# Agent attention with two expert layers: five weight buffers and six value buffers in place of four and seven, first queries loaded among the keys

## The chip, the cores and the metric

One core of one Trainium2 chip runs the kernel in one launch. The metric is the device time of that core in microseconds (us), the median of several runs. The engines are called PE (matrix multiplies, with its weight loads listed as PEld), DVE (vector), ACT (scalar), POOL (GpSimd) and SP (here only an issuer of transfers). Transfers are also issued from POOL and from ACT.

## What is computed

49 agents attend over 12,480 keys, then 12,480 queries attend over the agents, and the result runs through two expert layers with a squared ReLU. In short, with N = 12480, C = 128 and a hidden width of 2048:

```python
def sm(a, b):
    s = scale * (a @ b.T)
    e = np.exp(s - s.max(-1, keepdims=True))
    return e / (e.sum(-1, keepdims=True) + 1e-09)
agent_v = sm(agents, k) @ v                # 49 x 128
x = sm(q, agents) @ agent_v                # 12480 x 128
r = np.maximum(x @ w_in, 0.0)              # 12480 x 2048
x = (moe_s * (r * r) + moe_b) @ w_out
h = np.maximum(x @ w_in2, 0.0)
out = (h * h @ w_out2)
```

q, k, v and the agents are 32-bit floats, the weights 64-bit floats. [...]

## The kernel before

Everything is written in one hand-made order (`tc.manual_schedule`): the order of the Python statements is the order of the instructions on each engine, and the order of the transfers on each issuer.

The kernel has four stages.

- **Keys** (the loop `for g in range(NG + 1)`). The 12,480 keys come in 13 groups, twelve of 1024 rows (512 KB) and a last one of 192 rows. In step g, `k_transpose(g)` turns group g on PE (L412) and ACT copies the result (L414), `k_scores(g - 1)` multiplies by the agents on PE (L422) and ACT copies the scores into S (L424), and `k_max(g - 2)` keeps a running maximum on DVE (L428). `k_load(g + KB - 1)` issues the key group five ahead from SP (L369); KB = 6 buffers hold raw keys.
- **The maximum** (from `k_max(NG - 1)`): DVE reduces the running maximum (L452), then in the order of PE's queue come `q_transpose(0)` (L145), the transpose of the maximum (L456), `q_transpose(1)`, a small multiply that spreads the maximum to all partitions (L464). DVE copies its result to `mb` (L466).
- **Values** (the loop with L507): per group, DVE subtracts `mb` from S (L490), ACT takes the exponential (L491), PE multiplies by the value group. `v_upto(min(g + VB, NG))` issues further value groups from SP (L376). A value group lies in buffer `v_buf[g % VB]`.
- **Experts**: 28 blocks of queries, 8 steps a block, from about 75 us to the end.

Weights are 16 chunks of 512 KB, numbered w0 to w15 here. `w_load` (L251 for two of the matrices, L256 for the other two) brings a chunk into one of RAW buffers, `w_decode` takes it apart with an ACT instruction (L268) and DVE instructions (L270 to L285) that stand between the instructions of the other stages: `fill(n)` puts n of them in. A chunk's raw buffer is free after L280. `next_load()` issues the next chunk from POOL when a decoding has ended, as far as `fill` counts. So the raw buffers say how many chunks are on their way ahead of the decoder.

`FIRST` is the string that lists the first transfers of SP's queue, "k" for a key group and "w" for a weight chunk; there are as many "w" as raw buffers. After it, SP's transfers come as the loops write them: before the change k6 in step 1, k7 in step 2 and so on to k12 in step 7, v0 in step 7, v1 in step 8, q0, q1 and v2 in step 9, v3 to v6 in steps 10 to 13, and the others in the value loop. In step 2, ACT issues two small broadcasts, `s_sb` and `b_sb`.

Of the kernel before, what the change touches and what calls it, by code (L numbers as in the profile page):

```python
# [18 lines left out]
BP = 112  # L19
LAG = 2  # L20
WC = 512
RAW = 4
KB = 6
VB = 7
FIRST = "kkwkwkwkwk"

FILL_K = (1, 3, 4, 4, 4, 5, 5, 5, 5, 5, 5, 4, 1, 0)
FILL_T = 1
# [15 lines left out]
def tile_agent_attention_two_moe(  # L44
# [40 lines left out]
    def rows_of(x, piece):  # L85
        t, p, j = piece
        return x[t:t + p * j, :].rearrange("(p j) c -> p j c", j=j)
# [34 lines left out]
    def tokens_of(x, t):  # L122

        t0, p, j = blocks[t]
        if t < DIRECT:
            return rows_of(x, blocks[t])
        return x[t0:t0 + p * j, :].rearrange("(j p) c -> p j c", j=j)

    def q_load(t):
        t0, p, j = blocks[t]  # L130
        q_raw[t] = qp.tile([P, 512], F32, tag="q_raw", name="q_raw", bufs=3)
        if t < DIRECT:
            nc.sync.dma_start(out=q_raw[t].rearrange("p (j c) -> p j c", c=C)[:p, :j], in_=tokens_of(q, t))
        else:
            with nc.allow_non_contiguous_dma(reason="channels on the partitions"):
                nc.sync.dma_start(out=q_raw[t][:, :p * j], in_=q[t0:t0 + p * j, :].rearrange("t c -> c t"))
# [105 lines left out]

    raw_p = ctx.enter_context(tc.tile_pool(name="raw_p", bufs=RAW))
    dec_p = ctx.enter_context(tc.tile_pool(name="dec_p", bufs=3))
# [61 lines left out]
    def fill(n):  # L306

        for _ in range(n):
            if len(running) < 2 and ready and (not running or running[0][1] >= 3):
                running.append([ready.pop(0), 0])  # L310
            if not ready and loaded and (not running or running[-1][1] >= ZA):
                raw, i, pair = loaded.pop(0)
                sl = slice(i * WC, (i + 1) * WC)
                g = w_decode(raw, pair[0][:, sl], pair[1][:, sl])
                next(g)
                ready.append(g)
            if not running and ready:
                running.append([ready.pop(0), 0])
            if not running:
                while late:  # L320
                    late.pop(0)[1]()
                    undone[0] -= 1
                return
            for x in late:
                x[0] -= 1
            while late and late[0][0] <= 0:
                late.pop(0)[1]()
                undone[0] -= 1
            r = running.pop(0)
            r[1] += 1  # L330
            try:
                next(r[0])
                running.append(r)
            except StopIteration:
                done.append(0)
            for i in range(len(done)):
                done[i] += 1
            if done and done[0] > 2:
                done.pop(0)
                next_load()  # L340
# [14 lines left out]
    with tc.manual_schedule():  # L355

        with tc.tile_pool(name="pre", bufs=1) as pre, tc.tile_pool(name="kp", bufs=2) as kp:
            NG = len(kblocks)
            ag = pre.tile([NA, C], F32, name="ag")
            vs = {}  # L360
            v_buf = [pre.tile([P, 8, C + 1], F32, name=f"v{i}") for i in range(VB)]
            S = pre.tile([P, NT, NA], F32, name="S")
# [3 lines left out]
            def k_load(g):  # L366
                _, p, j = kblocks[g]
                kraw[g] = kp.tile([P, 8, C], F32, tag="kraw", name="kraw", bufs=KB)
                nc.sync.dma_start(out=kraw[g][:p, :j], in_=rows_of(k, kblocks[g]))  # L369

            def v_upto(n):
                while len(vs) < n:
                    g = len(vs)
                    _, p, j = kblocks[g]
                    vs[g] = v_buf[g % VB]
                    nc.sync.dma_start(out=vs[g][:p, :j, :C], in_=rows_of(v, kblocks[g]))  # L376
# [11 lines left out]
            for x in Xs:  # L388
                nc.gpsimd.memset(x.bitcast(F32), 0.0)
            for what in FIRST:  # L390
                if what == "k":
# [15 lines left out]
            def k_transpose(g):  # L407
                _, p, j = kblocks[g]
                x = kraw.pop(g)
                ps = ps_h.tile([P, 1024], F32, tag="h", name="ps_k")  # L410
                for i in range(j):
                    nc.tensor.transpose(out=ps[:, i * p:(i + 1) * p], in_=x[:p, i], identity=ident[:p, :p])  # L412
                kT[g] = kp.tile([P, 1024], F32, tag="kT", name="kT")
                nc.scalar.copy(kT[g][:, :p * j], ps[:, :p * j])  # L414

            def k_scores(g):
                _, p, j = kblocks[g]
                x = kT.pop(g)
                ps = ps_m.tile([P, 512], F32, tag="m", name="ps_ks")
                sc = ps[:p, :j * GAP].rearrange("p (j n) -> p j n", n=GAP)  # L420
                for i in range(j):
                    nc.tensor.matmul(out=sc[:, i], lhsT=x[:, i * p:(i + 1) * p], rhs=aT, start=True, stop=True)  # L422
                to = S[:p, t0[g]:t0[g] + j]
                nc.scalar.copy(to, sc[:, :, :NA])  # L424

            def k_max(g):
                _, p, j = kblocks[g]
                nc.vector.tensor_tensor(  # L428
                    out=mxa[:p, :j], in0=S[:p, t0[g]:t0[g] + j], in1=(mxa if g > 1 else S)[:p, :j], op=ALU.max
                )  # L430

            for g in range(NG + 1):
                if g < NG:
                    k_transpose(g)
                if g and g + KB - 1 < NG:
                    k_load(g + KB - 1)
                if g == 2:
                    nc.scalar.dma_start(out=s_sb, in_=s.partition_broadcast(P))
                    nc.scalar.dma_start(out=b_sb, in_=b.partition_broadcast(P))
                if g == 9:  # L440
                    q_load(0)
                    q_load(1)
                v_upto(min(g - KB, VB))
                fill(FILL_K[g])
                if g:
                    k_scores(g - 1)
                if g > 2:
                    k_max(g - 2)
# [43 lines left out]

            v_upto(VB)
            for g in range(3):
# [4 lines left out]
            for g, (_, p, j) in enumerate(kblocks):  # L499
# [6 lines left out]
                for i in range(j):  # L506
# [6 lines left out]
                    )  # L513
                v_upto(min(g + VB, NG))
                fill(FILL_V[g])
# [190 lines left out]
```

## Time and profile before

| what | value |
|---|---|
| median of three runs | 1127.05 us (1122.84, 1127.05 and 1130.47) |
| the profiled execution | 1124.37 us, of it a span of 1122.4 us from the first to the last instruction |
| busy shares of the span | PE 99%, PEld 91%, DVE 86%, ACT 85%, POOL 1% |
| keys, PE | from 5.2 to 39.9 us |
| values, PE | from 46.5 to 70.6 us |
| expert stage | from 75.3 us to the end |
| transfers of the first 73 us | 16 weight chunks, 13 key groups, 13 value groups, 5 query blocks |

The span is counted from the first instruction. A transfer's "landing" is the time from its issue on the queue until its completion is seen. An idle time in a row of the timeline is the time that the engine stood still ahead of that row, with what ended it. The share of a clock of 1.00 is TensorE's upper level of 2.4 GHz, 0.50 its lower level of 1.2 GHz.

### The profile page before, as it was taken

What the parts mean: (1) busy time and instruction counts of PE and PEld (TensorE: products, weight loads), DVE (VectorE), ACT (ScalarE), POOL (GpSimd) and SP (SyncE); (2) the same over time, 40 slices, a digit from 0 to 9 for tenths busy, and PEclk for the clock granted to TensorE, in tenths of its full rate; (3) what the DMA queues carried; (4) which work ended last, traced back from release to release, by engine and by line L of the source; (5) the groups of instructions that cost most, each with busy time, mean ns of one, the idle gap of its engine ahead of it and who ended that gap; (6) DMA issues with size and microseconds to landing.
All of it is one profiled execution on the core that took longest, in us unless ns stands there. A gap on an engine that the chain in (4) does not pass through costs nothing.

```text
span 1122.4 us, 15479 instructions
## 1 busy us (share of the span) xinstructions
PE 1105.9 (99%) x5787; PEld 1021.1 (91%) x5787; DVE 964.3 (86%) x1426; ACT 949.8 (85%) x1196; POOL 12.4 (1%) x36
## 2 busy tenths in 40 slices
PE   9988999999999999999999999999999999999998
PEld 8877999999999999999999999999999999999997
DVE  6889888888888888888888888888888888888876
ACT  6669888888888888888888888888888888888876
POOL 2100000000000000000000000000000000000000
PEclk9899999999999999999999999999999999999999
DMA  9960039999999999999999999999999999800000
GB/s 343 291 166 1 1 19 7 15 15 15 7 16 15 16 9 14 15 15 15 8 15 15 15 8 15 15 15 8 15 15 15 8 15 15 12 1 9 9 10 15
DMA packets 1282674, 34.96 MB, mean 31 GB/s; under 512 B 1255255, under 2 KB 1277672, under 8 KB 1282600
## 3 DMA queue, kind: packets, MB, share of 16 engines
q1 hardware_dynamic: 1280320, 27.56, 116.1%
q0 software_dynamic: 1728, 6.29, 1.7%
q8 instruction: 45, 0.74, 0.4%
q14 instruction: 29, 0.24, 0.2%
q10 hardware_dynamic: 552, 0.12, 0.1%
HBM read 27.58 MB, written 6.39 MB: 30 GB/s over the span
## 4 chain that ended last, share of the span: by engine, by line
PE 93%; DMA 3%; DVE 1%; ACT 1%; issue 0%; SPq 0%; DVEq 0%; ACTq 0%
PE ps_y L584 47%; PE ps_h L572 24%; PE ps_h L562 16%; PE ps_av L507 2%; DMA kraw<-in_k_dram 2%; DMA q_raw<-in_q_dram 2%; PE ps_o L623 1%; PE ps_sT L181 1%; PE ps_x L227 0%; DVE gl L117 0%; PE ps_b L196 0%; PE ps_s L171 0%; ACT r L551 0%; PE ps_q L145 0%; ACT r L552 0%
## 5 line engine op out<-in xcount | busy, mean ns | idle before, releaser
L117 DVE TENSOR_TENSOR gl<-r,gh 128x896 fp32r<-128x896 f32 (+2 forms) x450 | 487.7, 1084 | 16.8 <-ACT gh L116 1.5
L551 ACT ACTIVATE r<-ps_h 128x896 f32<-128x896 f32 (+2 forms) x450 | 408.9, 909 | 98.8 <-PE ps_h L562 79.7
L552 ACT ACTIVATE r<-r 128x896 f32<-128x896 f32 (+2 forms) x450 | 427.0, 949 | 14.3
L116 DVE CAST gh<-r 128x896 fp32r<-128x896 f32 (+2 forms) x445 | 276.7, 622 | 112.5 <-ACT r L552 100.6
L562 PE MATMUL ps_h<-X,Ml 113*128 113x448 f32 (+1 forms) x448 | 166.5, 372 | 2.5 <-DVE X L238 1.7
L572 PE MATMUL ps_h<-yh,wi2l 128*128 128x448 f32 (+1 forms) x448 | 168.8, 377 | 0.2 <-ACT r L551 0.2
L584 PE MATMUL ps_y<-gh,wol 128*128 128x448 f32 (+1 forms) x448 | 163.0, 364 | 0.9 <-ACT y L592 0.9
L562 PE MATMUL ps_h<-X,Mh 113*128 113x448 f32 (+1 forms) x448 | 163.5, 365 | 0.0
L584 PE MATMUL ps_y<-gl,woh 128*128 128x448 f32 (+1 forms) x448 | 162.6, 363 | 0.6 <-DVE gl L117 0.6
L572 PE MATMUL ps_h<-yl,wi2h 128*128 128x448 f32 (+1 forms) x448 | 163.2, 364 | 0.0
L572 PE MATMUL ps_h<-yh,wi2h 128*128 128x448 f32 (+1 forms) x448 | 163.2, 364 | 0.0
L584 PE MATMUL ps_y<-gl,wo2h 128*128 128x448 f32 (+1 forms) x448 | 162.4, 362 | 0.1
L584 PE MATMUL ps_y<-gh,woh 128*128 128x448 f32 (+1 forms) x448 | 162.4, 362 | 0.0
L584 PE MATMUL ps_y<-gh,wo2l 128*128 128x448 f32 (+1 forms) x448 | 162.3, 362 | 0.0
L584 PE MATMUL ps_y<-gh,wo2h 128*128 128x448 f32 (+1 forms) x448 | 161.8, 361 | 0.0
L562 PEld LDWEIGHTS ps_h<-X,Ml 113*128 113x128 f32 x448 | 84.3, 188 | 9.3 <-issue 3.3
L584 PEld LDWEIGHTS ps_y<-gh,wol 128*128 128x128 f32 x448 | 84.4, 188 | 7.3 <-ACT y L592 1.2
L572 PEld LDWEIGHTS ps_h<-yl,wi2h 128*128 128x128 f32 x448 | 84.8, 189 | 6.5 <-DVE yl L117 0.2
L584 PEld LDWEIGHTS ps_y<-gl,woh 128*128 128x128 f32 x448 | 84.4, 188 | 6.7 <-DVE gl L117 0.9
L572 PEld LDWEIGHTS ps_h<-yh,wi2h 128*128 128x128 f32 x448 | 84.1, 188 | 7.0
L572 PEld LDWEIGHTS ps_h<-yh,wi2l 128*128 128x128 f32 x448 | 84.2, 188 | 6.7 <-ACT r L551 0.5
L562 PEld LDWEIGHTS ps_h<-X,Mh 113*128 113x128 f32 x448 | 84.9, 190 | 5.2
(125 smaller groups left out, 975.6 us busy)
## 6 DMA issues: line engine op xcount, KB each, us to landing
kraw<-in_k_dram SPq DMA_DIRECT2D x12, 512.0 KB, 11.6
v<-in_v_dram SPq DMA_DIRECT2D x12, 512.0 KB, 7.9
q_raw<-in_q_dram SPq DMA_DIRECT2D x27, 224.0 KB, 36.3
out_dram<-o SPq DMA_DIRECT2D x27, 224.0 KB, 2.8
raw<-in_moe_w_out_dram POOLq DMA_DIRECT2D x8, 512.0 KB, 8.3
raw<-in_moe_w_in_dram SPq DMA_DIRECT2D x4, 512.0 KB, 8.1
raw<-in_moe_w_in_dram POOLq DMA_DIRECT2D x4, 512.0 KB, 8.0
q_raw<-in_q_dram SPq DMA_DIRECT2D x1, 192.0 KB, 31.7
```

The lines of the kernel that those rows point to most:

```text
L116: copy(dst[0], src)
L117: eng_lo.tensor_tensor(out=dst[1], in0=src, in1=dst[0].bitcast(F32), op=ALU.subtract)
L181: nc.tensor.matmul(out=ps[:KS, :n], lhsT=aS, rhs=x[z][:, :n], start=(z == 1), stop=(z == 0))
L507: nc.tensor.matmul(out=ps_av[:NA, :C + 1], lhsT=S[:p, t0[g] + i], rhs=vs[g][:p, i], start=(g == 0 and i == 0), stop=(g == NG - 1 and i == ...
L551: nc.scalar.activation(r[:, c, :n], ps[:, c, :n], AF.Relu)
L552: nc.scalar.activation(r[:, c, :n], r[:, c, :n], AF.Square)
L562: nc.tensor.matmul(out=ps[:, c, :n], lhsT=M[z][:KS, sl], rhs=X[t], start=(z == 1), stop=(z == 0))
L572: nc.tensor.matmul(out=ps[:, c, :n], lhsT=w[:, sl], rhs=y[:, :n], start=(z == 0), stop=(z == 2))
L584: nc.tensor.matmul(out=py[t][:, :n], lhsT=wz[:, m], rhs=g[:, c, :n], start=(m == 0 and z == 0), stop=(m == NCH - 1 and z == 2),)
L623: nc.tensor.transpose(out=po[:, i], in_=x[:, (h * jh + i) * p:(h * jh + i + 1) * p], identity=ident)
```

## The change

Three constants and two lines of the key loop are edited. RAW goes from 4 to 5 and `FIRST` gets an eleventh entry, a fifth weight chunk (w4) behind k5; it was the first chunk that POOL issued, and POOL now begins with w5. VB goes from 7 to 6. In the key loop the values are issued two steps sooner, one a step from step 5 on (v0) to step 10 (v5), and the two first query blocks in steps 7 and 8 in place of both in step 9.

```diff
-RAW = 4
+RAW = 5
 KB = 6
-VB = 7
-FIRST = "kkwkwkwkwk"
+VB = 6
+FIRST = "kkwkwkwkwkw"
@@ in the key loop
-                if g == 9:
-                    q_load(0)
-                    q_load(1)
-                v_upto(min(g - KB, VB))
+                if g in (7, 8):
+                    q_load(g - 7)
+                v_upto(min(g - 4, VB))
```

SP's order of transfers, before and after (step numbers in brackets):

```
before: k0 k1 w0 k2 w1 k3 w2 k4 w3 k5    [1]k6 [2]k7 [3]k8 [4]k9 [5]k10 [6]k11 [7]k12 v0 [8]v1 [9]q0 q1 v2 [10]v3 ...
after:  k0 k1 w0 k2 w1 k3 w2 k4 w3 k5 w4 [1]k6 [2]k7 [3]k8 [4]k9 [5]k10 v0 [6]k11 v1 [7]k12 q0 v2 [8]q1 v3 [9]v4 [10]v5
```

The order of the decoding instructions among the others on DVE and ACT is the same in both kernels: it depends on `fill`'s numbers, and a loaded chunk is at hand for it in the list with four as with five.

## Rows read from the trace of the kernel before

**Rows 1.** Busy time of each engine by stretch, with TensorE's granted clock
```profile
core 0: us, PE busy (x) PEld busy (x) DVE busy (x) ACT busy (x) POOL busy (x), PEclk, DMA share, GB/s
20.00:23.73 3.73, 2.82 (x26) 2.71 (x25) 1.65 (x5) 0.75 (x2) 0.35 (x1) 1.00 1.03 384
...
40.00:42.00 2.00, 0.00 (x0) 0.00 (x0) 1.74 (x4) 0.23 (x2) 0.00 (x0) 1.00 1.20 267
43.30:50.10 6.80, 6.77 (x31) 6.10 (x32) 5.36 (x16) 3.46 (x7) 0.00 (x0) 0.50 1.04 278
...
100.00:1100.00 1000.00, 998.99 (x5058) 922.92 (x5057) 869.07 (x1227) 870.69 (x1070) 0.00 (x0) 1.00 1.26 12
```

**Rows 2.** Timeline of PE: start, duration, line, operation, count, idle before
```profile
20.02 1.06 PE L412 MATMUL ps_k<-ident,kraw 128*128 128x128 f32 x8
...
23.73 1.07 PE L412 MATMUL ps_k<-ident,kraw 128*128 128x128 f32 x8 [0.91 <-DMA kraw<-in_k_dram]
...
34.86 1.05 PE L412 MATMUL ps_k<-ident,kraw 128*128 128x128 f32 x8
...
37.48 0.34 PE L412 MATMUL ps_k<-ident,kraw 96*128 96x96 f32 x2
...
42.04 0.57 PE L145 MATMUL ps_q<-ident,q_raw 112*128 112x112 f32 x4 [2.13 <-DMA q_raw<-in_q_dram]
...
44.15 0.66 PE L464 MATMUL ps_mb<-dm,ones_r 49*128 49x49 f32 x2
...
54.06 16.58 PE L507 MATMUL ps_av<-v,S 128*49 128x129 f32 x148
```

**Rows 3.** Timeline of SP: issues of the key groups 7, 8 and 12
```profile
8.67 0.33 SPq L369 DMA_DIRECT2D kraw<-in_k_dram  x1
...
12.50 0.33 SPq L369 DMA_DIRECT2D kraw<-in_k_dram  x1
...
21.12 0.34 SPq L369 DMA_DIRECT2D kraw<-in_k_dram  x1
```

**Rows 4.** Transfers by issue: the same three groups, with us to landing
```profile
kraw<-in_k_dram SPq DMA_DIRECT2D x1, 512.0 KB, 14.9
...
kraw<-in_k_dram SPq DMA_DIRECT2D x1, 512.0 KB, 13.9
...
kraw<-in_k_dram SPq DMA_DIRECT2D x1, 96.0 KB, 12.5
```

**Rows 5.** Waits of SP's queue, 9 to 14 us: total, times, longest
```profile
SPq L369 <- DMA raw<-in_moe_w_in_dram: 3.4, 1, 3.4
```

**Rows 6.** Timelines of POOL and ACT: chunk w4, issued and first read
```profile
12.28 0.88 POOL L256 DMA_DIRECT2D raw<-in_moe_w_out_dram  x1 [8.20 <-DVE x L273]
...
22.98 0.66 ACT L268 ACTIVATE z<-raw 128x512 f32<-128x512 f32 x1 [3.49 <-DMA raw<-in_moe_w_out_dram]
```

**Rows 7.** Transfer queues (q1 SP, q0 POOL), 20 to 22 us: packets, MB, share
```profile
q1 hardware_dynamic: 111, 0.39, 50.9%
q0 software_dynamic: 103, 0.37, 50.2%
```

**Rows 8.** The same queues, 31 to 32 us, while SP's queue moves values
```profile
q0 software_dynamic: 69, 0.27, 80.8%
q1 hardware_dynamic: 82, 0.05, 19.4%
```

**Rows 9.** SP's queue alone, 30 to 38 us: packets, MB, share of 16 engines
```profile
q1 hardware_dynamic: 1860, 1.14, 56.9%
```

**Rows 10.** Chain that ended last, 25 to 42 us: start, duration, what
```profile
25.04 16.86 DMA q_raw<-in_q_dram
```

**Rows 11.** Timeline of DVE between the keys and the values
```profile
41.82 0.68 DVE L285 SCALAR_TENSOR_TENSOR wol<-z,ex 128x512 fp32r<-128x512 f32 x1
...
43.08 0.24 DVE L460 TENSOR_SCALAR dm<-ident,mt 49x49 f32<-49x49 f32 x1
```

**Rows 12.** The page's list of transfers: count, KB each, median us to landing
```profile
v<-in_v_dram SPq DMA_DIRECT2D x12, 512.0 KB, 7.9
```

## The prediction

> **What bounds the kernel now.** I read the table of stretches first. From 100 to 1100 us PE is busy for 998.99 of 1000 us at the full clock [rows 1]. The change leaves these instructions as they are, so a gain or a loss can only arise in the first 75 us, and as the order of every engine is fixed, a shift of the first expert step passes to the end one for one. That also caps the answer: one per cent is 11.3 us, and the whole front has only a few idle microseconds. (One per cent is about what a measurement of this kernel can tell from no change.)
>
> Next, PE's timeline over the front. In the key stage PE goes from group to group every 2.62 us (group 11 at 34.86, group 12 at 37.48) and has one hole, 0.91 us ahead of group 7, which waited for its keys [rows 2]. Between keys and values it has a second one of 2.13 us, ended by q0 [rows 2], whose transfer fills the chain from 25.04 to 41.9 us [rows 10]. Soon behind this hole the granted clock is at 0.50 for 6.8 us [rows 1]. In the value stage 148 multiplies take 16.58 us without a hole [rows 2]. So three things could be won: 0.9 us at group 7, about 1 us at q0, and up to 3.4 us of clock.
>
> Then the transfers, as the change only moves transfers. The queues are full in the key stage: from 20 to 22 us SP's and POOL's queues have 50.9% and 50.2% of the engines' time, 0.39 and 0.37 MB [rows 7]. Group 7 was issued at 8.67 and landed 14.9 us later, at 23.6; group 8 was issued at 12.50 and landed at 26.4 [rows 3, 4]. A transfer takes its turn in SP's queue; one 512 KB turn in this stretch is 26.4 - 23.6 = 2.8 us. The reader is to see that keys arrive hardly sooner than PE wants them: group 6 started at 20.02 without a wait, group 7 had one [rows 2].
>
> **The change part by part.**
>
> *Chunk w4 from SP, behind k5.* Its issue goes from POOL (0.88 us there, off any path) to SP, and its landing from about 22.9 (ACT waited for it 3.49 us at L268 [rows 6]) to the turn that group 6 had, before 20.02. ACT's wait goes. But POOL doesn't fall silent: its next issue needs the raw buffer of w0, as the one at 12.28 did [rows 6], and so w5 comes exactly where w4 came, and POOL's traffic runs beside SP's as before. Chunk w4 is thus 512 KB more in front of group 6. Group 6 takes group 7's turn (landing 23.6), group 7 takes group 8's (26.4) [rows 3, 4]. PE wants group 6 at 20.02 and stands until 23.6, then does group 6 in 2.62 us, and group 7 starts at 26.4 in place of 23.73 [rows 2]: **+2.7 us**. Lower bound: at the 0.76 MB in 2 us that both queues moved together [rows 7], 0.52 MB are 1.4 us if POOL gives way; then group 7 lands at 25.0, +1.3. Upper bound: a whole turn for group 6 with no wait of group 7 saved, 3.6. I take 2.7, since the turns are read from the very places that are exchanged.
>
> Here the Trainium skill bears on the change: "DMA: Bandwidth & Descriptors", section "Issuing engines are not separate DMA queues", says that transfers started by different engines run on the same 16 DMA engines and interleave, so moving an issue brings no bandwidth. The two half shares in rows 7 agree with it. By the rule, w4 sooner is bought from the keys, and the sum would keep its first term; only a second path for transfers would take it out.
>
> *What this stall does to the clock.* PE would idle for about 3.5 us at 20 us. An idle of 0.9 us left the clock at 1.00, one of 2.1 us at 40 us was followed by 6.8 us at 0.50 [rows 1, 2]. So I expect the lower level in groups 6 to 8. At 0.50 for 6.8 us PE does 3.4 us less work, the upper bound; a short fall, or one in which PE waits for group 7 anyway, costs nothing, the lower bound. I take the middle, **+1.7 us**.
>
> *Values v0 and v1 ahead of k11 and k12.* Each issue on SP also waits for the one eight transfers before it among those of SP and ACT: group 8 waited 3.4 us for weight chunk w2 [rows 5], with which it shares no buffer, and which is eight before it in the order. After the change this puts k11 behind k6's landing (23.6), v0 behind w4, v1 behind k7 (26.4), k12 behind the small s: all before their turn in the queue, so no term; s and b on ACT move by one lane too, b behind w2, which ACT's next L268 waits for in any case. The turn itself is the cost. Group 12 landed at 21.12 + 12.5 = 33.6 and was wanted at 37.48 [rows 2 to 4], a slack of 3.9 us, and with the terms above it is wanted at 37.48 + 4.4 = 41.9. In front of it there are now w4, v0 and v1, 1.57 MB. At the pace of SP's queue from 30 to 38 us, 1.14 MB in 8 us [rows 9], that is 11 us: landing 44.6, late by 2.7. At 0.38 MB per us [rows 7] it is 4.1 us: landing 37.7, not late. POOL's loads are called by the decoder, whose DVE instructions stand behind the late maxima, so POOL leaves more to SP than before; I take a value near the lower end, **+0.5 us** (0 to 2.7).
>
> Why the pace is so low: from 31 to 32 us, with values on SP's queue, POOL's 69 packets carried 0.27 MB and SP's 82 packets 0.05 MB [rows 8]; with keys, 103 and 111 packets carried nearly the same [rows 7]. Small packets lose. The Trainium skill ("DMA: Bandwidth & Descriptors", "Queues, rings and completion order") has each DMA engine switch between queues packet by packet; the rows agree, and the rule speaks against values in front of keys, whose price by it is the upper end above.
>
> *q0 and q1 in steps 7 and 8.* q0 now follows k12 directly. `q_transpose(0)` stands ahead of the transpose of the maximum on PE, so PE no longer waits there. What is late next is DVE: its decoding instruction L285 runs from 41.82 to 42.5 ahead of the maximum's reduction, and the `dm` that PE needs ended at 43.3; PE began L464 only at 44.15, behind `q_transpose(1)` [rows 2, 11]. With q0 there, `dm` ends at about 43.0 and L464 starts then: **-1.1 us**. Bounds: 0 (q0 or q1 late as before; q1 has v2 in front of it now) and -2.1 (the whole wait).
>
> *Six value buffers.* A group that waits for a free buffer is now issued five groups ahead of its use, before six. A group takes 16 multiplies, 16 x 16.58/148 = 1.8 us [rows 2], so five give 9.0 us; the median landing is 7.9 [rows 12]. Six give 10.8. Hidden with 1.1 us to spare, 0 us; if the landing took 10 us it would cost about 1 us, once. Values two steps sooner win nothing, since the value stage had no wait for one.
>
> *The clock behind the keys.* If PE idles less between keys and values, the 6.8 us at 0.50 [rows 1] may go: 0 to -3.4 us. Some idle stays (the last maximum and its reduction), so I take 0.
>
> Sum: 2.7 + 1.7 + 0.5 - 1.1 = **+3.8 us**. The profiled execution took 1124.37 us, so 1128.2 by its own time. It lies 2.7 us below the median of the three runs, which differ by 7.6 us; against the median the forecast is 1127.05 + 3.8 = **1130.8 us**.
>
> **The rivals.**
>
> *Keys not late (ends faster).* If group 6 lands by 20.0 with w4 in front of it, because the full queue is no limit there, the 0.9 us at group 7 and 1.1 us at q0 are won, and 3.4 us more if the clock stays up: -2.0 to -5.4, 1121.7 to 1125.0 us. For it: 0.91 us is all that keys were late so far, and w4 leaves POOL's queue. Against it: the exchange of turns above. It decides at PE's start of group 6: at 20.0 or at 23.6. Chance 0.20.
>
> *Late keys, but no low clock behind them.* Terms as forecast with the 6.8 us at full clock: 3.8 - 3.4 = +0.4, 1127.5 us. For it: q0 fills the hole. Against it: reductions remain between keys and values. Chance 0.24.
>
> *Values starve the keys.* The upper ends of clock and of k12: 2.7 + 3.4 + 2.7 - 1.1 = +7.7, 1134.8 us. For it: rows 8. Against it: POOL's loads are put off too. Chance 0.14.
>
> *Values late for lack of the seventh buffer.* About +1 to +2 on top, 1132 to 1133 us. Against it: the first six are all on their way before the stage begins. Chance 0.06.
>
> The forecast itself has 0.36.
>
> **How the numbers follow.** Likeliest 1130.8; its own range, from the bounds of its terms one at a time, 1127 to 1134. The range takes in the second and third rivals, and most of the first: 1121.5 to 1136.5. None of the cases reaches one per cent (below 1115.8 or above 1138.3); I leave 0.02 for faster, 0.03 for slower (two of the costs at once), 0.95 within.
>
> **What would show it.** PE's group 6 starting near 23.6 with a wait on keys shows the first step, the clock row from 23 to 30 us the second; a wait of PE on keys ahead of groups 11 or 12 the third; PE's wait on q0 gone, L464 some 3 us after the last scores (they end at 39.9 now) rather than 4.2, the fourth; no wait on values the fifth. ACT's 3.49 us at w4 must go in any case. The prediction is wrong if group 6 starts on time, or if the key stage ends at the same 39.9 us.

## The result, and the profile after

The changed kernel takes 1133.36 us (median of six runs, 1130.89 to 1136.09) where the kernel before takes 1124.74 (six runs, three more than were shown). The ratio is 1.0071, 95% interval 1.0058 to 1.0083: slower by 0.71%, 8.6 us at the medians. The interval is a quarter of one per cent wide, so a change well below the one per cent that the prediction named can be told here. It is slower by less than one per cent, as forecast, and 1133.4 lies in the range; but the loss is more than twice the likeliest +3.8 us. That it lies in the range so clearly is in part luck: the median of three runs to which the forecast was added, 1127.05, is 2.3 us above the median of six. Added to 1124.74, the forecast's own range (1127 to 1134) would end at 1131.7, and only the wide one, with the rivals in it, would still hold the result (up to 1134.2). The profiled execution took 1133.1 us with a span of 1130.9, 8.5 us more than the span before.

The timeline of PE in the changed kernel (start, duration, line, operation, count, idle before). Lines after the edited loop are one lower, so L463 is the L464 of before, and L506 the L507.

```profile
18.45 1.06 PE L412 MATMUL ps_k<-ident,kraw 128*128 128x128 f32 x8 [1.63 <-DMA kraw<-in_k_dram]
...
24.31 1.66 PE L412 MATMUL ps_k<-ident,kraw 128*128 128x128 f32 x8 [3.06 <-DMA kraw<-in_k_dram]
...
29.07 1.92 PE L412 MATMUL ps_k<-ident,kraw 128*128 128x128 f32 x8
...
40.68 1.04 PE L412 MATMUL ps_k<-ident,kraw 128*128 128x128 f32 x8
...
45.96 0.60 PE L145 MATMUL ps_q<-ident,q_raw 112*128 112x112 f32 x4 [0.24 <-ACT S L424]
...
48.85 0.66 PE L463 MATMUL ps_mb<-dm,ones_r 49*128 49x49 f32 x2 [0.28 <-DVE dm L459]
...
74.22 2.39 PE L506 MATMUL ps_av<-v,S 128*49 128x129 f32 x20 [0.89 <-DMA v<-in_v_dram]
```

The first four rows are groups 5, 6, 7 and 11 of the keys. Groups 6, 7 and 11 answer to 20.02, 23.73 and 34.86 [rows 2]: they are 4.3, 5.3 and 5.8 us late, and group 6 waits 3.06 us for its keys. Group 5 waits too, 1.63 us, which was not foreseen. The next two are the first query block and L463: the wait for q0 is gone, and L463 comes at 48.85 in place of 44.15, 4.7 us late. The last row is value group 11: PE waits 0.89 us for it, where the value stage of before had no hole.

The chain that ended last says what that wait hung on: start, duration, what.

```profile
64.51 9.57 DMA v<-in_v_dram
```

v11 took 9.6 us from its issue to its landing.

The table of stretches with TensorE's clock (columns as in [rows 1]) shows four stretches at 0.50:

```profile
24.70:31.40 6.70, 6.70 (x35) 6.70 (x33) 2.73 (x6) 2.90 (x5) 0.40 (x1) 0.50 1.03 386
48.60:55.30 6.70, 6.45 (x30) 6.10 (x31) 6.03 (x17) 3.47 (x7) 0.15 (x1) 0.50 0.17 43
89.60:92.80 3.20, 3.20 (x8) 2.69 (x9) 3.17 (x6) 1.78 (x4) 0.00 (x0) 0.50 0.03 5
106.60:109.90 3.30, 3.30 (x13) 2.90 (x12) 3.20 (x7) 2.81 (x4) 0.00 (x0) 0.50 0.00 0
```

Before, there were two. One is the 6.8 us from 43.3 us on [rows 1]; the other lies in the expert stage, and the prediction says nothing of it:

```profile
84.30:87.60 3.30, 3.30 (x11) 2.86 (x10) 3.27 (x7) 2.36 (x5) 0.00 (x0) 0.50 0.02 5
```

Both are still there, 5.3 us later. The first and the last of the four are new. The view of the cores gives the mean over the whole span, first for the kernel before, then for the changed one:

```profile
core 0: 1122.4 us, clock 0.995
```

```profile
core 0: 1130.9 us, clock 0.991
```

1122.4 x 0.005 = 5.6 us of full clock were lost before, 1130.9 x 0.009 = 10.2 us after. The stretches make up nearly all of it: half of 10.1 us before, half of 19.9 us after.

Last, the transfers: SP's issue of w4 and its landing, then those of k6 and of k7, and ACT's first reading of w4.

```profile
7.10 0.39 SPq L256 DMA_DIRECT2D raw<-in_moe_w_out_dram  x1
...
raw<-in_moe_w_out_dram SPq DMA_DIRECT2D x1, 512.0 KB, 14.6
...
8.60 0.34 SPq L369 DMA_DIRECT2D kraw<-in_k_dram  x1
...
kraw<-in_k_dram SPq DMA_DIRECT2D x1, 512.0 KB, 15.6
...
12.40 0.33 SPq L369 DMA_DIRECT2D kraw<-in_k_dram  x1
...
kraw<-in_k_dram SPq DMA_DIRECT2D x1, 512.0 KB, 14.6
...
21.76 0.66 ACT L268 ACTIVATE z<-raw 128x512 f32<-128x512 f32 x1 [1.14 <-DMA raw<-in_moe_w_out_dram]
```

w4 landed at 7.10 + 14.6 = 21.7 us, k6 at 8.60 + 15.6 = 24.2, k7 at 12.40 + 14.6 = 27.0. The places where k7 and k8 had landed, 23.6 and 26.4 [rows 3, 4], are those of k6 and k7 now, as the prediction had it, each 0.6 us later. What was bought with it is little: ACT reads w4 at 21.76 in place of 22.98, and still waits 1.14 us for it, where it waited 3.49 [rows 6].

Where the 8.5 us of span arise, read from where PE's steps start: 5.8 at key group 11, back to 4.7 at L463, 4.6 at the first value (51.09 for 46.50), 6.0 at the first expert multiply (81.24 for 75.28), 8.5 at the end.

### The profile page after: what moved, and what is told of

The parts are those of the page before. It is cut to its first block, busy times and chain, and to the rows that moved or that the text cites. A ratio compares the mean times of both kernels' runs of the same rounds, so it can differ in the third digit from the quotient of the medians.

```text
span 1130.9 us, 15478 instructions
## 1 busy us (share of the span) xinstructions
PE 1110.5 (98%) x5787; PEld 1025.0 (91%) x5787; DVE 964.0 (85%) x1426; ACT 950.3 (84%) x1196; POOL 11.6 (1%) x34
## 4 chain that ended last, share of the span: by engine, by line
PE 93%; DMA 3%; ACT 2%; DVE 2%; issue 1%; SPq 0%; DVEq 0%; ACTq 0%
PE ps_y L583 46%; PE ps_h L571 24%; PE ps_h L561 15%; DMA kraw<-in_k_dram 2%; PE ps_av L506 1%; PE ps_ks L422 1%; PE ps_o L622 1%; PE ps_sT L181 1%; DMA v<-in_v_dram 1%; ACT r L550 1%; PE ps_k L412 1%; ACT r L551 1%; PE ps_x L227 0%; DVE gl L117 0%; PE ps_b L196 0%
## 6 DMA issues: line engine op xcount, KB each, us to landing
raw<-in_moe_w_out_dram SPq DMA_DIRECT2D x1, 512.0 KB, 14.6
```

## The experiments

Theory of the turns: w4, 512 KB more in front of k6, makes the keys late, and PE's idle time brings the clock down. Its rivals: the values ahead of the keys and the lost seventh buffer; and the two broadcasts s and b, whose packets pass from 13 to 20 us, while w4 is on its way (the trace of before shows them too, the prediction had not read them). All ratios are to the kernel before on the same chip, 0.1% being 1.1 us.

### Which part of the change costs it

**w4 alone** (with six value buffers):

```diff
-RAW = 4
+RAW = 5
-VB = 7
+VB = 6
-FIRST = "kkwkwkwkwk"
+FIRST = "kkwkwkwkwkw"
```

> The kernel before with the fifth weight buffer and w4 behind k5 on SP's queue (and six value buffers, without which it has no room); queries and values are issued where they were before. Theory of the turns (w4's 512 KB push k5 to k7 back, PE stands, the clock falls): nearly the whole loss, +5 to +7 us against before, group 6 on PE at 23.5 to 24.5 us, clock at 0.50 soon after, no wait for q0. Rival, values ahead of keys and six buffers: the loss stays away, at most +2 us, group 6 at 20 to 21 us.

Ratio 1.0084 (1.0069 to 1.0099): the whole loss, more than the 5 to 7 us expected. PE's timeline at key groups 6 and 11 and in the value stage:

```profile
23.34 1.06 PE L412 MATMUL ps_k<-ident,kraw 128*128 128x128 f32 x8 [2.58 <-DMA kraw<-in_k_dram]
...
41.33 1.04 PE L412 MATMUL ps_k<-ident,kraw 128*128 128x128 f32 x8
...
59.31 16.65 PE L507 MATMUL ps_av<-v,S 128*49 128x129 f32 x148
```

Group 6 waits 2.58 us for keys and comes a little sooner than the 23.5 us expected, and group 11 is 6.5 us late, with queries and values where they were. The value stage has no hole.

**Queries and values sooner, without w4** (six value buffers, four weight buffers):

```diff
-VB = 7
+VB = 6
-                if g == 9:
-                    q_load(0)
-                    q_load(1)
-                v_upto(min(g - KB, VB))
+                if g in (7, 8):
+                    q_load(g - 7)
+                v_upto(min(g - 4, VB))
```

> The kernel before with the queries in steps 7 and 8, the values two steps sooner and six value buffers; four weight buffers, w4 from POOL as before. Theory of the turns: groups 6 and 7 on PE as before (20.0 and 23.7 us), group 12 late by 0 to 3 us, the wait for q0 gone (-1.1 us), -1 to +2 us in all. Rival, values ahead of keys: group 11 or 12 late by 3 us or more, and +4 us or more in all.

Ratio 1.0028 (1.0014 to 1.0041), 2 to 3 us (2.3 at the medians), between the two expectations. Groups 6 and 11 and L463:

```profile
20.60 1.04 PE L412 MATMUL ps_k<-ident,kraw 128*128 128x128 f32 x8
...
34.44 1.04 PE L412 MATMUL ps_k<-ident,kraw 128*128 128x128 f32 x8
...
43.77 0.42 PE L463 MATMUL ps_mb<-dm,ones_r 49*128 49x49 f32 x2
```

Group 6 has no wait and group 11 is on time, so in this execution the values do not starve the keys. But k12 lands only at 38.1 us (issued at 26.02 and 12.0 us on its way), just as PE takes it at 38.20; its slack of 3.9 us is gone. The profiled execution shows no loss (L463 at 43.77, its span 1121.9 us), as it is the fastest of twelve that reach from 1123.7 to 1132.5. Where the other eleven lose their 2 to 3 us no trace shows, and a late k12 is not ruled out; it stays open.

**Six value buffers alone:**

```diff
-VB = 7
+VB = 6
```

> The kernel before with six value buffers in place of seven, and nothing else. Theory of the turns: -0.5 to +1 us, PE waits for no value group or for less than 1 us. Rival, the seventh buffer was needed: PE waits for values in several groups, +2 us or more.

Ratio 1.0010 (0.9998 to 1.0021): no change that can be told. Key group 5 and most of the value stage:

```profile
17.84 1.06 PE L412 MATMUL ps_k<-ident,kraw 128*128 128x128 f32 x8 [0.97 <-DMA kraw<-in_k_dram]
...
52.75 16.69 PE L507 MATMUL ps_av<-v,S 128*49 128x129 f32 x148
```

No hole in the values. And group 5 waits 0.97 us for its keys here, though nothing ahead of it was touched, and with w4 alone it has no wait: the 1.63 us at group 5 in the changed kernel need be no sign of the change, as the start of an execution varies by about that much.

The parts do not add up to the whole: 0.84% for w4 and 0.28% for queries and values are more than the 0.71% of both together. Each is known to about 0.15%, and why the second does not show on top of the first stays open.

### What the stall is made of

**The changed kernel with the broadcasts put off:**

```diff
-                if g == 2:
-                    nc.scalar.dma_start(out=s_sb, in_=s.partition_broadcast(P))
-                    nc.scalar.dma_start(out=b_sb, in_=b.partition_broadcast(P))
...
         total = NB * NPR
+        nc.sync.dma_start(out=s_sb, in_=s.partition_broadcast(P))
+        nc.sync.dma_start(out=b_sb, in_=b.partition_broadcast(P))
```

> The changed kernel with the two small broadcasts s_sb and b_sb issued from SP ahead of the expert steps in place of from ACT in step 2. Theory of the turns: w4's 512 KB still stand in front of k6, only at the full pace of 0.4 MB per us, so group 6 on PE at 21.5 us or later and +4 us or more against before. Rival, the broadcasts' small packets slow the queues from 13 to 18 us and w4 only falls into that time: group 6 on PE before 21 us, the clock stays at 1.00 there, and at most +2 us against before.

Ratio 1.0046 (1.0031 to 1.0062). Key group 6, and the clock after it:

```profile
22.32 1.94 PE L412 MATMUL ps_k<-ident,kraw 128*128 128x128 f32 x8 [2.88 <-DMA kraw<-in_k_dram]
...
21.30:34.80 13.50, 12.48 (x60) 12.52 (x61) 7.48 (x16) 5.25 (x9) 1.10 (x2) 0.50 1.07 365
```

Group 6 still waits 2.88 us, and comes at 22.3. So w4's turn costs without the broadcasts too. The changed kernel is faster without them by 0.71 - 0.46 = 0.25%, 2.8 us (the two intervals just overlap), and k6 is 13.8 us on its way in place of 15.6. This profile is the slowest of its six runs; its low clock lasts 13.5 us.

**The kernel before with the broadcasts put off** (the same edit):

> The kernel before with the two small broadcasts s_sb and b_sb issued from SP ahead of the expert steps in place of from ACT in step 2. If their packets are what slows the queues from 14 to 20 us: the 0.9 us wait of PE at group 7 goes, SP's and POOL's queues move 0.35 MB per us or more between 15 and 18 us where they moved 0.2, and -1 to -2 us against before. If the dip has another cause: no change of the dip, 0 us within 1 us.

Ratio 0.9981 (0.9972 to 0.9990), 2.1 us faster. Transfers by queue from 15 to 18 us (q1 SP, q0 POOL, q10 ACT: packets, MB, share), in the kernel before:

```profile
q1 hardware_dynamic: 174, 0.63, 63.1%
q0 software_dynamic: 16, 0.07, 16.9%
q10 hardware_dynamic: 183, 0.00, 3.1%
```

and with the broadcasts put off:

```profile
q1 hardware_dynamic: 220, 0.77, 66.1%
q0 software_dynamic: 93, 0.38, 34.7%
```

183 packets that carry next to nothing (the two broadcasts are 1 KB together) go with 0.70 MB in 3 us; without them it is 1.15 MB. The dip was theirs. Key group 11 comes 1.6 us sooner for it than its 34.86 [rows 2]:

```profile
33.23 1.05 PE L412 MATMUL ps_k<-ident,kraw 128*128 128x128 f32 x8
```

So the broadcasts slow both kernels, and are not what the change costs: with them put off in both, the changed kernel is slower by 1.0046 / 0.9981 = 1.0065, about as much as with them (1.0071).

**PE kept busy in the changed kernel**, with spare transposes whose result nothing uses:

```diff
             for g in range(NG + 1):
+                if g in (5, 6):
+                    ps = ps_y.tile([P, 512], F32, tag="y2", name="ps_d")
+                    for i in range(12 if g == 5 else 22):
+                        nc.tensor.transpose(out=ps[:, :P], in_=ident, identity=ident)
                 if g < NG:
                     k_transpose(g)
```

> The changed kernel with 12 spare transposes on PE ahead of group 5 and 22 ahead of group 6, in the time in which PE waits for keys (their result is used by nothing). Keys land as late as in the changed kernel, but PE does not idle. If the low clock in the key stage is a cost of its own (about 3 us): the clock stays at 1.00 from 24 to 31 us, group 11 on PE at 37 to 38.5 us in place of 40.7, and +4.5 to +6.5 us against before. Rival, the keys' landings bind group by group, clock or not: group 11 at 40 us or later, +8 us.

Ratio 1.0053 (1.0038 to 1.0068). Key groups 6 and 11, `q_transpose(1)` and value group 11, then the stretch that had been at 0.50 and the one behind the keys:

```profile
25.55 1.09 PE L412 MATMUL ps_k<-ident,kraw 128*128 128x128 f32 x8 [1.46 <-DMA kraw<-in_k_dram]
...
38.91 1.04 PE L412 MATMUL ps_k<-ident,kraw 128*128 128x128 f32 x8
...
47.90 0.98 PE L145 MATMUL ps_q<-ident,q_raw 112*128 112x112 f32 x4 [1.37 <-DMA q_raw<-in_q_dram]
...
75.88 4.04 PE L510 MATMUL ps_av<-v,S 128*49 128x129 f32 x20 [2.29 <-DMA v<-in_v_dram]
...
24.70:31.40 6.70, 5.79 (x51) 5.68 (x52) 4.59 (x11) 4.14 (x7) 0.55 (x1) 1.00 1.03 383
45.70:55.70 10.00, 8.20 (x36) 7.25 (x37) 7.67 (x21) 3.69 (x8) 0.51 (x1) 0.50 0.54 146
```

The clock stays at 1.00, and PE goes from group 6 to group 11 in 13.4 us where it took 16.4 in the changed kernel: the low clock was 3.0 us of the key stage, the late keys the other 2.8 of its 5.8. Group 11 itself, at 38.9 in place of 40.7 (37 to 38.5 were expected), shows only 1.8 of the 3.0, because in this execution SP's transfers run late from the start, long before the spare transposes: k6 was issued at 9.68 us in place of 8.60, and landed 1.3 us later, at 25.5. Part of the gain is given back: PE waits 1.37 us for q1, which has v2 in front of it, and 2.29 us for v11, and the low clock behind the keys lasts 10 us in place of 6.7. This profile is the slowest of its six runs, with a span longer than the changed kernel's (1132.3 us); the median is 2.7 us shorter (1130.7 for 1133.4). The intervals of this ratio and the changed kernel's overlap, so at the end of the run a gain of some 2 us is likely, not shown.

**Both, PE busy and broadcasts put off** (6 and 22 transposes):

> The changed kernel with the broadcasts ahead of the expert steps and 6 and 22 spare transposes on PE ahead of groups 5 and 6. What is left is the turn of w4 alone: if turns, broadcasts and clock add up, group 6 on PE at 22.3 us, group 11 at 35.5 to 37 us, +1 to +3 us against before. Rival, the keys stay late behind w4 and the values whatever the clock: group 11 at 40 us or later, +5 us.

Ratio 1.0028 (1.0018 to 1.0038). Key groups 6 and 11 and `q_transpose(1)`:

```profile
22.95 1.09 PE L412 MATMUL ps_k<-ident,kraw 128*128 128x128 f32 x8
...
36.30 1.04 PE L412 MATMUL ps_k<-ident,kraw 128*128 128x128 f32 x8
...
45.47 0.57 PE L145 MATMUL ps_q<-ident,q_raw 112*128 112x112 f32 x4 [1.36 <-DMA q_raw<-in_q_dram]
```

Group 11 is 1.4 us late, where it was 5.8. The two gains add up: 0.71 less 0.25 (broadcasts) less 0.18 (clock, 0.71 - 0.53) is 0.28, as measured, though each is known to about 0.15 only. The broadcasts slow the kernel before too; against that kernel with its broadcasts put off, group 11 is 3.1 us late here (36.30 for 33.23) and the ratio 1.0028 / 0.9981 = 1.0047. So what is left of the change at the full clock is 3.1 us of late keys in the key stage, and behind it PE's 1.36 us wait for q1.

### Another place for w4

**Behind k8:**

```diff
-FIRST = "kkwkwkwkwkw"
+FIRST = "kkwkwkwkwk"
...
                 if g and g + KB - 1 < NG:
                     k_load(g + KB - 1)
+                if g == 3:
+                    next_load(nc.sync)
```

> The changed kernel with w4 issued from SP in step 3, behind k8, in place of behind k5. Theory of the turns: groups 6 to 8 keep their turns, group 6 on PE at 20 to 21 us, group 7 at 23 to 24 us, no low clock in the key stage from 24 to 31 us; groups 9 to 12 have slack; +1 to +4 us against before (what is left are the values ahead of keys). Rival, a fifth chunk in flight slows everything wherever it stands: +6 us or more.

Ratio 1.0091 (1.0079 to 1.0103): as bad, and the expectation of +1 to +4 us failed. ACT's first reading of w4 and the PE step that it held up:

```profile
28.86 0.66 ACT L268 ACTIVATE z<-raw 128x512 f32<-128x512 f32 x1 [9.41 <-DMA raw<-in_moe_w_out_dram]
...
30.85 3.68 PE L422 MATMUL ps_ks<-aT,kT 128*128 128x64 f32 x16 [6.67 <-ACT kT L414]
```

Groups 6 and 7 are on time (20.3 and 23.1), but w4 now lands too late for the decoder. ACT stands 9.4 us in front of L268, its copy of the next transposed keys is queued behind that, and PE idles 6.7 us for the copy. Before, the same wait was 3.49 us [rows 6]. Neither of the two places that were tried in SP's queue is free: behind k5 w4 makes the keys late, behind k8 it is late itself.

**From POOL at the start:**

```diff
-                    next_load(nc.sync)
+                    next_load(nc.sync if len(loaded) < 4 else nc.gpsimd)
```

> The changed kernel with w4 issued at the start from POOL in place of from SP behind k5; it is still the fifth chunk, only in the other queue and in 4 KB packets rather than 1 KB. If the bytes alone count: group 6 on PE at 23 us or later, +7 us or more against before. If w4's place in SP's queue and its 1 KB packets cost the most (SP moved little beside POOL's 4 KB packets while w4 was its turn): group 6 at 20 to 22 us and +2 to +5 us.

Ratio 1.0060 (1.0048 to 1.0072). POOL's issue of w4, then key group 6:

```profile
4.01 0.88 POOL L256 DMA_DIRECT2D raw<-in_moe_w_out_dram  x1
...
24.54 1.91 PE L412 MATMUL ps_k<-ident,kraw 128*128 128x128 f32 x8
```

Group 6 comes at 24.5, as in the changed kernel, though w4 never was in SP's queue. So it is the bytes that cost, and hardly the queue: the loss is 6.5 us, a little under the 7 expected of the bytes alone, and the ratios 1.0060 and 1.0071 can't be told apart. That is what the Trainium skill says ("DMA: Bandwidth & Descriptors", "Issuing engines are not separate DMA queues"): whoever starts a transfer, it runs on the same DMA engines.

### What could be won

**Queries sooner alone:**

```diff
-                if g == 9:
-                    q_load(0)
-                    q_load(1)
+                if g in (7, 8):
+                    q_load(g - 7)
```

> The kernel before with the queries issued in steps 7 and 8, each ahead of the value group of its step, and nothing else. Theory: q0 lands before the keys end, L464 starts 3 us after the last scores rather than 4.2: -1 us, and -1 to -4 us if the clock no longer falls behind the keys. Rival, the wait for q0 is covered by the maximum anyway: 0 us within 0.7 us.

Ratio 0.9997 (0.9987 to 1.0008): nothing. The multiply that spreads the maximum and the first 48 of the values:

```profile
43.42 0.66 PE L463 MATMUL ps_mb<-dm,ones_r 49*128 49x49 f32 x2
...
45.77 8.16 PE L506 MATMUL ps_av<-v,S 128*49 128x129 f32 x48
```

The wait for q0 is gone, L463 comes 0.7 us sooner, but the first 48 value multiplies take 8.16 us: the low clock covers more of them.

**Queries sooner and broadcasts put off:**

> Both edits on the kernel before: queries in steps 7 and 8, broadcasts ahead of the expert steps. If both waits (0.9 us at group 7, 1.1 us at q0) are real and apart: -2 us, down to -5 us if the clock stays up behind the keys. If one covers the other: -1 us.

Ratio 0.9983 (0.9974 to 0.9992), the same as the broadcasts alone. The first 48 value multiplies:

```profile
44.27 7.68 PE L503 MATMUL ps_av<-v,S 128*49 128x129 f32 x48
```

**The same, with PE kept busy ahead of the maximum:**

```diff
             q_transpose(0)
+            ps = ps_y.tile([P, 512], F32, tag="y2", name="ps_d")
+            for i in range(10):
+                nc.tensor.transpose(out=ps[:, :P], in_=ident, identity=ident)
             fill(FILL_T)
```

> The kernel before with the queries in steps 7 and 8, the broadcasts ahead of the expert steps, and 10 spare transposes on PE between the first query block and the transpose of the maximum. If the idle time of 1.3 us there brings the low clock of the value stage: no 0.50 between 41 and 49 us, -4 to -6 us against before. Rival, what follows idles enough all the same: the low clock stays, -2 us.

Ratio 0.9982 (0.9968 to 0.9996). The first 48 value multiplies, then two stretches with their clock, and last the stretch of the expert stage at 0.50 without the spare transposes:

```profile
43.70 5.49 PE L506 MATMUL ps_av<-v,S 128*49 128x129 f32 x48 [0.59 <-issue]
...
41.00:48.00 7.00, 6.14 (x54) 5.77 (x54) 6.54 (x19) 3.47 (x7) 0.18 (x1) 1.00 1.08 274
78.60:85.30 6.70, 5.82 (x15) 5.06 (x16) 5.39 (x11) 5.19 (x7) 0.00 (x0) 0.50 0.01 2
...
83.00:86.20 3.20, 3.20 (x10) 2.83 (x10) 3.17 (x5) 2.50 (x4) 0.00 (x0) 0.50 0.02 5
```

There is no low clock in the values any more and the 48 take 5.49 us rather than 7.68; the first expert multiply comes at 71.1 us, 2.4 us sooner than without the spare transposes (73.5). But the low clock of the expert stage lasts 6.7 us in place of 3.2, and the span is only 1.3 us shorter; the medians, 1122.2 and 1122.6, can't be told apart, and the 4 to 6 us expected did not come. The three kernels with four weight buffers and the broadcasts put off beat both kernels, and no more than the broadcasts alone.

## Why the prediction was right and where it was short

**Right: what decides.** The first term, w4's 512 KB in front of the keys, is the cause: the first experiment has the whole loss with it and nothing of the rest but the sixth buffer, which alone costs nothing that can be told. The test that was named, group 6 near 23.6 us with a wait on keys, came out at 24.3. That POOL's next chunk comes exactly where w4 came held too: POOL issued w5 at 12.16 us. The first rival (keys not late) is out. ACT's wait for w4 was to go; 1.14 us of it are left, since w4 landed at 21.7 and not before 20.0.

**Right: the turn, +2.7 us.** k6 and k7 took the landings of k7 and k8, 0.6 us late. From group 6 to group 11 PE needs 13.4 us at the full clock (the run with PE kept busy); from 24.31 on that gives 37.7 for group 11, 2.8 us late. This is an estimate from two executions; with the broadcasts put off in both kernels the same difference is 3.1.

**Mis-sized: the clock in the key stage, +1.7 us.** 6.7 us at 0.50 came where they were expected, and cost 3.0 (40.68 less 37.7). The term was the middle between 3.4 and nothing, the latter in case PE waited for group 7 anyway. It did not: k7 landed at 27.0, while PE, at the low clock, was at group 6 until 29.07 and busy in all 6.70 us of the stretch.

**Not needed: values ahead of keys, +0.5 us.** PE waited for no keys at groups 11 and 12. k12 landed at 38.9 (29.77 and 9.1 us), 5.2 us later than before, but it was wanted 5.8 us later, at 43.3. So the rival "values starve the keys" is out for the changed kernel's profile; without w4, where PE is not late, it stays open, as said at the second experiment.

**Right: q0, -1.1 us.** The delay shrinks from 5.8 us at group 11 to 4.7 at L463. That it is worth nothing alone (ratio 0.9997) the prediction had only as a bound.

**Mis-sized: six value buffers, 0 us.** 9.0 us from issue to use were set against a median landing of 7.9 [rows 12]; v11 landed after 9.6. With the 0.89 us wait, the value stage grew by 1.4 us (first value to first expert multiply, 4.6 to 6.0 us late). It was the last rival, with 0.06. That the lost buffer is the reason is argued, not shown: v11 was late in the changed kernel, by 2.29 us with PE kept busy and by 3.13 with w4 behind k8, but with six buffers there was no such wait with w4 alone, with w4 from POOL, or with the kernel before around them, and no run has the changed kernel with seven. A median hides the one transfer that decides.

**Wrong: a shift passes to the end one for one, and only the first 75 us count.** The delay grew from 6.0 us at the first expert multiply to 8.5 at the end. The new stretch at 0.50 from 106.6 to 109.9 us is 1.6 us of that, a longer wait of PE on DVE at L227 0.6 (1.37 us for 0.77). The step holds where the low clock of the expert stage is as before: with w4 from POOL the delay goes from 6.1 us to 5.9, with the queries sooner alone from 0.2 to 0.6. Where a further stretch comes, about 25 us after the first expert multiply, the delay grows by 1.4 us or more, with w4 alone from 5.3 to 6.7. It is no mark of a late front: the profiles with six value buffers alone and of the kernel before with the broadcasts put off have it too (from 99.6 and 97.5 us), though their experts begin sooner than before, by 0.7 and 2.9 us. What makes the clock fall there in some executions is not settled.

Sum of what was off: +1.4 in the key stage (5.8 for 2.7 + 1.7, nearly all of it the clock), -0.5 for keys behind values, -0.1 up to the first value, +1.4 in the values, +2.5 in the experts is 4.7, and 3.8 + 4.7 = 8.5 us.

## What to carry to other kernels

When the queues are full, a deeper prefetch is not sooner for free: price it as one more transfer in front of what is wanted next, at the rate that the queues have in that very stretch, and look for who stands behind the one that becomes late. A hole on PE can cost twice, once for the wait and once for the low clock after it: here 2.8 us for the late keys and 3.0 for the clock. Small broadcasts that nobody needs soon belong behind the stretch in which the transfers bind.

## What the runs showed of the hardware that was not expected

Two broadcasts of 0.5 KB each are hundreds of packets of a few bytes, and while 183 of them passed, the other queues moved 0.70 MB in 3 us in place of 1.15. Putting them off made the kernel before 0.19% faster (0.10 to 0.28), more than any part of the change won.

Keeping PE busy with ten spare transposes took the low clock out of the value stage, and the one in the expert stage became longer, 6.7 us in place of 3.2. The mean clock of the profiled executions rose from 0.995 to 0.997, and the medians differ by 0.4 us, which can't be told from nothing.
